# Transposing x in blocks of two tokens of one head, with the states doubled in place of a copy that pairs heads

## The chip, the cores and the metric

The kernel runs on one core of a Trainium2 chip. A core has five engines with queues of their own: TensorE (PE in the profile; its weight loads have a row of their own, PEld), VectorE (DVE), ScalarE (ACT), GpSimd (POOL) and SyncE (SP, which here only issues DMAs). TensorE reads SBUF and writes PSUM, eight banks of 2 KB per partition. The metric is the device time of one execution in microseconds (us). Inputs are float32, the arithmetic is bfloat16 with sums in float32.

## The reference

There are B = 8 batches, H = 8 heads, S = 512 tokens, Ns = 32 states, and D = 64 elements per head. A block of cross attention between tokens and states is followed by a feed-forward layer with an exact GELU.

```python
scores = scale * x @ state^T          # per batch and head: 512 x 32
a = exp(scores - max); a /= a.sum(-1) + 1e-09
xread = a @ state                     # 512 x 64
scores2 = scale * state @ x^T         # 32 x 512, softmax over the tokens
sread = a2 @ x                        # 32 x 64
attn = concat([xread, sread], axis=2) # 544 rows per batch and head
x = attn, heads side by side          # (8 * 544) x 512
out = gelu(x @ w_in) @ w_out          # w_in 512 x 2048, w_out 2048 x 512
```

## The kernel before, in words

The order of the work is written out by hand (`tc.manual_schedule()`): each engine runs its instructions in the order in which the code issues them, and waits on semaphores where data come from another engine or a DMA. There is no planner.

**Per batch.** For the rows of tokens the kernel never forms xread. It multiplies each head's states with that head's 64 rows of w_in first (`p_mm`, L435: the tile `P`, 32 states of 4 heads = 128 rows, for two groups of heads t = 0, 1, by 2048 columns) and then multiplies the transposed attention weights `AT` with P (`mm1`, L501, called as `M`): a block of 128 of the 2048 hidden columns by 512 tokens, two matmuls of 512 columns, then one GELU on ScalarE into `g`. The heads are numbered h = 4 t + c, with t the half (0 or 1) and c = 0 to 3. The second product, g by w_out, is made for batches 1 to 7 with seven half-size products in place of eight (`X(b, "1")` to `X(b, "7")`, L672), whose operands are sums and differences that VectorE makes (`g_sum`, L629, and `w_diff`, L563); one quarter of that is cut once more (`sub_a`, `sub_b`, L736 and L743). Results leave by DMAs from SyncE's queue.

**Scores and softmax.** `scores(b, half)` (L325) makes 8 matmuls of 64 columns: the stationary operand is a 128 x 128 block of x transposed, the moving operand 64 columns of `sbd`, a table of the states in which two 64 x 32 blocks stand on a diagonal and the rest is zero. The exponential on ScalarE follows, and `norm` on VectorE (a sum, a reciprocal, and a product of two SBUF operands: L353, L355, L356). The state reads (`reads_mm`, L955) need x with a column of ones beside it, `xo`, which `rearr_ones` (L230) copies from x.

**How x comes in.** `load_x(b)` (L115) is a DMA issued from GpSimd's queue that converts to bfloat16. It fills `xb`: 128 partitions, 8 heads, and per head 4 tokens of 64 elements side by side. There are two buffers. In `scores` a block of x transposed holds one token of two heads, c of t = 0 and c of t = 1. In `xb` the 64 elements of those two heads lie far apart. So `rearr(b)` (L221) copies them together into `x4` on GpSimd, two copies of 1024 elements per partition for each of batches 2 to 7, and `xtr_dma(b)` (L276) transposes x4 into `xT` by one DMA transpose from SyncE's queue. Batch 1 is transposed on TensorE (`xtr`, L264): 32 transposes of 64 columns each, into the two partition halves of PSUM, and two copies by VectorE. Batch 0 has a path of its own.

**How the states come in.** `load_st` (L120) loads the states of batch 1, of batch 2, and of batches 3 to 7 at three places, as `st_bf`: 128 partitions (4 heads by 32 states), the two halves t side by side. `state_prep(b0, b1)` (L156) makes one TensorE transpose for each batch and two VectorE copies into the diagonal blocks of `sbd`; it is called for batch 1 at L1134, batch 2 at L1187, and batches 3 to 7 together at L1218. `sbd` is set to zero once at the start on GpSimd (L95).

**The order around the change.** Batches 0 and 1 are woven together by hand (L1074 to L1220). From there each batch b = 2 to 7 has eight slots p = 0 to 7 (loop at L1222). Every slot holds two blocks of M and one product X of the batch before; the scores of the next batch stand in slot 1, its softmax in 2 and 3, the DMA transposes in 3 and 5, its P and state reads in slot 5 (`p_all`, L986, copies at L1002), the small products of `sub_a` and `sub_b` in 5 and 6. GpSimd's queue carries loads and copies; a one-element copy `hold_for` (L1015) makes it wait for a given block of g, so that a load doesn't start earlier. PSUM tiles named "f" take four buffers in turn, the others fixed banks.

**Other uses of the buffers.** The two x4 buffers later hold sums of w_in for the rows of states (`sr_w`, L814, products "1" and "6") and the last sum of g (L1320).

Of the kernel before, what the change touches and what calls it, by code (L numbers as in the profile page):

```python
# [17 lines left out]
def kernel(  # L18
# [49 lines left out]
    ident = persist.tile([128, 128], BF16, name="ident")  # L68
    sbd = persist.tile([128, B, HC, 2 * NS], BF16, name="sbd")
    XSR = persist.tile([128, HC, NS, B], BF16, name="XSR")  # L70
# [4 lines left out]
    x0b = persist.tile([128, 4, SJ, 2, D], BF16, name="x0b", tag="mix1")  # L75
    xT0 = persist.tile([128, 4, SJ, 128], BF16, name="xT0", tag="mix2")
    sb0 = persist.tile([128, 2, 2, 2, NS], BF16, name="sb0")
    hold = persist.tile([128, 1], BF16, name="hold")
    spare = persist.tile([128, 1], FP32, name="spare")
    warm = persist.tile([128, 512], BF16, name="warm")  # L80
    xos = [persist.tile([128, SJ, HC, 132], BF16, name=f"xo_{i}") for i in range(2)]
    x4s = [persist.tile([128, SJ, HC, 128], BF16, name=f"x4_{i}") for i in range(2)]

# [10 lines left out]

    nc.gpsimd.memset(sbd, 0.0)  # L95
    xbs = {}
# [37 lines left out]
    def load_rest():  # L134
        load_w_out(4, 6)
        load_w_out(6, 8)
        load_w_in(1024, 1536)
        load_w_out(8, 12)
        load_w_in(1536, 2048)
        load_st(2, 3)  # L140
        load_x(2)
        load_w_out(12, 16)
        load_x(3)


# [8 lines left out]


    def state_prep(b0, b1, pool=ps_f, tag="f"):  # L156
        n = b1 - b0
        ps = pool.tile([128, n, HC, NS], BF16, name="st_ps", tag=tag)
        for b in range(b0, b1):
            nc.tensor.transpose(  # L160
                ps[:, b - b0, :, :].rearrange("p c n -> p (c n)"),
                st_bf[:, b, :, :].rearrange("q t d -> q (t d)"),
                ident,
            )
        for t in range(2):
            nc.vector.tensor_copy(
                out=sbd[64 * t:64 * t + 64, b0:b1, :, 32 * t:32 * t + 32].rearrange(
                    "d b c n -> d (b c) n"
                ),
                in_=ps[64 * t:64 * t + 64, :, :, :].rearrange("d b c n -> d (b c) n"),  # L170
            )
# [23 lines left out]
    def state0_p(ps):  # L195
        for t in range(2):
            h = slice(64 * t, 64 * t + 64)
            nc.scalar.copy(out=sbd[h, 0, :, 32 * t:32 * t + 32], in_=ps[h, 2, :, :])

# [6 lines left out]
    def begin(b):  # L206
        A = Att()
        atts[b] = A
        A.x4 = x4s[b % 2]
        A.xo = xos[b % 2]  # L210
        if b > 0:
            A.xT = att.tile([128, SJ, HC, 128], BF16, name="xT", tag="xT")

# [5 lines left out]


    def rearr(b, ts=(0, 1)):  # L221
        A = atts[b]
        src = xbs[b].rearrange("p (t c) (j d) -> p t c j d", t=2, d=D)
        for t in ts:
            nc.gpsimd.tensor_copy(  # L225
                out=A.x4[:, :, :, 64 * t:64 * t + 64].rearrange("p j c d -> p c j d"),
                in_=src[:, t],
            )

# [33 lines left out]

    def xtr(b, cs):  # L264
        A = atts[b]
        xv = xbs[b].rearrange("p (t c) (j d) -> p j c t d", t=2, d=D)
        ps = ps_f.tile([128, len(cs), SJ, 128], BF16, name="xT_ps", tag="f")
        for i, c in enumerate(cs):
            for j in range(SJ):
                for t in range(2):  # L270
                    nc.tensor.transpose(ps[64 * t:64 * t + 64, i, j, :], xv[:, j, c, t, :], ident)
        nc.vector.tensor_copy(
            out=A.xT[:, :, cs[0]:cs[0] + len(cs), :].rearrange("p j c n -> p c j n"), in_=ps
        )
# [50 lines left out]
    def scores(b, half):  # L325
        A = atts[b]
        if half == 0:
            begin_e(b)
        pt = ps_f.tile([128, SJ, 2, 2, NS], FP32, name="pt", tag="f")
        for ci in range(2):  # L330
            c = 2 * half + ci
            for j in range(SJ):
                nc.tensor.matmul(  # L333
                    pt[:, j, :, ci, :],
                    lhsT=A.xT[:, j, c, :],
                    rhs=sbd[:, b, c, :],
                    start=True,
                    stop=True,
                )
# [95 lines left out]
    def p_mm(b, f, tiles):  # L435
# [44 lines left out]
    def pmat00(h):  # L480
# [3 lines left out]
        for c in range(HC):  # L484
            for t in range(2):
                nc.tensor.matmul(
                    ps[t][32 * c:32 * c + 32, :],
                    lhsT=sbd[64 * t:64 * t + 64, 0, c, 32 * t:32 * t + 32],
                    rhs=w_in_bf[64 * t:64 * t + 64, c, 256 * h:256 * h + 256],
# [324 lines left out]
    def sr_w(name):  # L814
        if name in "52":
            homes = [opool.tile([128, 2, 512], BF16, name="srw", tag="osb") for _ in range(2)]
        elif name == "7":
            t = att.tile([128, 2, 2, 512], BF16, name="srw7", tag="xT")
            homes = [t[:, 0], t[:, 1]]
        else:  # L820
            t = x4s["16".index(name)].rearrange("p j c n -> p (j c n)")
            t = t.rearrange("p (g k f) -> p g k f", g=2, k=2)
            homes = [t[:, 0], t[:, 1]]
        (h0, k0), (h1, k1), op = G_SUMS[name]
# [307 lines left out]
    mm2_m(0, 0)  # L1132
    mm2_m(0, 1)
    state_prep(1, 2)  # L1134
    mm2_m(0, 2)
# [4 lines left out]
    begin(1)  # L1140
    xtr(1, (0, 1))
    xtr(1, (2, 3))
    sread(0)
# [31 lines left out]
    begin(2)  # L1175
    rearr(2)
    xtr_dma(2)
    begin(3)
    rearr(3)
    rearr_ones(3)  # L1180
# [31 lines left out]
    for f, t, ps in ((0, 1, p0), (0, 0, p0), (1, 0, p1)):  # L1212
        nc.vector.tensor_copy(out=Ps[2][:, t, f * 512:(f + 1) * 512], in_=ps[t])
    M(28, 29)
    hold_for(1, 12)
    rearr_ones(2)
    M(30, 31)
    state_prep(3, B)  # L1218
    snap(1, "c2", "c2", xs[1, 0])
    X(1, "4")  # L1220

    for b in range(2, B):  # L1222
        nb = b + 1
        for p in range(8):
# [68 lines left out]
            if p == 5:  # L1293
# [25 lines left out]
    X(b, "6")  # L1319
    g_sum(b, "3", x4s[0].rearrange("p j (u c) n -> p (j u) (c n)", u=2))  # L1320
    R("3")
# [35 lines left out]
```

## Time and profile before

| | before |
|---|---|
| median of 3 runs | 201.92 us (201.89 to 202.7) |
| the profiled execution | 202.25 us, span 200.3 us |
| TensorE busy | 193.9 us (97%) |
| VectorE busy | 155.1 us (77%) |
| ScalarE busy | 145.6 us (73%) |
| GpSimd busy | 48.1 us (24%) |
| pairing copies on GpSimd (L225) | 12 copies, 1040 ns each |
| transposes of x of batch 1 (L271) | 32, 1.08 us of the chain |
| transposes of the states (L160) | 1, 1 and 5 |

Times count from the start of the span. The profile of one execution is read in parts: busy time by engine; the chain, which goes back from the last instruction to what released it, and so on; groups of instructions with their mean time and what ended the idle time before them; and the timeline. The share of the span by engine is an average over stages. In a row of the timeline a number ahead of the brackets is the start, then the duration; the brackets hold the idle time of that engine just before and what ended it. A matmul's record is longer than the pace at which matmuls follow each other, since they are pipelined: a 128 x 128 transpose has a record of 219 ns, and eight of them take 0.45 us in the chain.

### The profile page before, as it was taken

The page shows a single profiled execution, that of the slowest core. Times are in us where ns is not written, and L with a number is a line of the kernel's source. Part 1 is how long each engine was busy: PE and PEld are TensorE (multiplying, and loading weights), DVE is VectorE, ACT ScalarE, POOL GpSimd, SP SyncE. Part 2 cuts the span into 40 slices and gives each one's busy share as a digit, 9 for nine tenths or more (in the row PEclk, how much of TensorE's full clock was granted, in tenths as well). Part 3 has the DMA queues.
Part 4 walks back from the last instruction along what each step waited for, and adds up shares of the span by engine and source line. Part 5 has one row for each costly group of instructions (what it writes and reads, how often), then busy time and mean ns, then how long its engine had stood idle before and what let it go on. Part 6 is the DMA issues. An engine that isn't in the chain of part 4 may idle for free.

```text
span 200.3 us, 5055 instructions
## 1 busy us (share of the span) xinstructions
PE 193.9 (97%) x2102; PEld 134.3 (67%) x2107; DVE 155.1 (77%) x279; ACT 145.6 (73%) x264; POOL 48.1 (24%) x65
## 2 busy tenths in 40 slices
PE   7899999999999999999999999999999999999993
PEld 2533544465767777767777787677776888878893
DVE  2963796969989769975997798849966897984863
ACT  3785577699896799569966997599948778775120
POOL 8972504543403444040504300030000000000000
PEclk9999999999999999999999999999999999999999
DMA  5999999976494959680797025420024010030044
GB/s 192 197 174 202 206 199 201 183 136 142 84 149 77 241 65 164 141 214 0 77 188 209 5 67 95 138 75 27 28 107 106 0 55 0 7 153 0 18 146 157
DMA packets 40567, 23.16 MB, mean 116 GB/s; under 512 B 21856, under 2 KB 39136, under 8 KB 40544
## 3 DMA queue, kind: packets, MB, share of 16 engines
q0 software_dynamic: 13984, 8.10, 29.9%
q1 hardware_dynamic: 25728, 14.22, 27.5%
q10 hardware_dynamic: 832, 0.52, 0.8%
q8 instruction: 16, 0.26, 0.5%
q14 instruction: 7, 0.06, 0.1%
HBM read 17.30 MB, written 8.91 MB: 131 GB/s over the span
## 4 chain that ended last, share of the span: by engine, by line
PE 86%; DMA 5%; POOL 4%; ACT 2%; issue 0%; DVE 0%; POOLq 0%
PE xp L647 36%; PE hp L506 26%; DMA xb<-in_x_dram 5%; PE xp L727 5%; PE op L548 3%; PE sp L866 3%; PE rp L932 3%; POOL w_in_bf L105 2%; PE op L532 2%; PE xp L773 2%; PE pt L333 2%; ACT P L1002 1%; PE p_ps L441 1%; PE sr L962 1%; POOL sbd L95 1%; POOL w_out_bf L113 1%
## 5 line engine op out<-in xcount | busy, mean ns | idle before, releaser
L513 ACT ACTIVATE g<-hp 128x512 bf16<-128x512 f32 x124 | 67.1, 614 | 17.0 <-PE hp L506 16.8
L506 PE MATMUL hp<-AT,P 128*128 128x512 bf16 x248 | 62.2, 379 | 0.0
L647 PEld LDWEIGHTS <-gsum 128*128 128x128 bf16 x416 | 40.4, 98 | 8.9 <-issue 0.4
L647 PE MATMUL xp<-ws,gsum 128*128 128x256 bf16 x320 | 38.2, 273 | 0.0
L506 PEld LDWEIGHTS <-P 128*128 128x128 bf16 x248 | 23.0, 98 | 19.4 <-ACT P L452 0.7
L647 PEld LDWEIGHTS <-g 128*128 128x128 bf16 x240 | 23.3, 98 | 4.8
L637 DVE TENSOR_TENSOR gsum<-g 128x2048 bf16<-128x2048 bf16 x14 | 17.0, 1218 | 0.6 <-ACT g L513 0.6
L225 POOL COPY x<-xb 128x1024 bf16<-128x1024 bf16 x12 | 12.2, 1044 | 18.5 <-DMA xb<-in_x_dram 18.5
L235 POOL COPY xo<-xb 128x1024 bf16<-128x1024 bf16 x12 | 12.2, 1043 | 14.1 <-PE sr L962 13.9
L647 PE MATMUL xp<-w_out_bf,g 128*128 128x256 bf16 x128 | 15.3, 273 | 0.0
L647 PE MATMUL xp<-ws,g 128*128 128x256 bf16 x112 | 13.4, 273 | 0.0
L1016 POOL COPY hold<-g 128x1 bf16<-128x1 bf16 x7 | 2.3, 334 | 42.9 <-ACT g L513 42.9
L666 DVE TENSOR_TENSOR c<-qb 128x256 f32<-128x256 f32 x6 | 2.6, 425 | 12.7 <-ACT qb L749 12.7
L548 PE MATMUL op<-w_out_bf,g 128*128 128x512 bf16 x44 | 11.0, 380 | 0.5 <-issue 0.3
L647 PE MATMUL xp<-w_out_bf,gsum 128*128 128x256 bf16 x96 | 11.5, 273 | 0.0
L666 DVE TENSOR_TENSOR oh<-xp,c 128x512 f32<-128x512 f32 x14 | 9.6, 686 | 2.4 <-PE xp L647 2.0
L1002 DVE CAST P<-p_ps 128x512 bf16<-128x512 f32 x15 | 9.4, 683 | 2.4 <-PE p_ps L441 2.4
L356 DVE TENSOR_TENSOR a<-e,ics 128x512 bf16<-128x512 bf16 x14 | 10.5, 750 | 0.5
L353 DVE TENSOR_REDUCE cs<-e 128x16 f32<-128x512 bf16 x14 | 9.5, 678 | 0.9 <-ACT e L340 0.9
L513 ACT ACT_TABLE_LOAD x7 | 9.0, 1283 | 0.1
L441 PE MATMUL p_ps<-w_in_bf,sbd 64*32 64x512 bf16 x248 | 9.0, 380 | 0.0
L637 DVE TENSOR_TENSOR gsum<-gsum,g 128x2048 bf16<-128x2048 bf16 x7 | 8.6, 1225 | 0.2
(155 smaller groups left out, 308.9 us busy)
## 6 DMA issues: line engine op xcount, KB each, us to landing
out_dram<-oh SPq DMA_DIRECT2D x15, 256.0 KB, 3.3
xb<-in_x_dram POOLq DMA_DIRECT2D x7, 512.0 KB, 7.1
out_dram<-oh SPq DMA_DIRECT2D x6, 512.0 KB, 3.1
w_in_bf<-in_moe_w_in_dram POOLq DMA_DIRECT2D x6, 256.0 KB, 11.7
out_dram<-osb SPq DMA_DIRECT2D x5, 256.0 KB, 3.0
w_out_bf<-in_moe_w_out_dram POOLq DMA_DIRECT2D x4, 256.0 KB, 7.8
w_out_bf<-in_moe_w_out_dram POOLq DMA_DIRECT2D x2, 512.0 KB, 13.3
x0f<-in_x_dram SPq DMA_DIRECT2D x3, 256.0 KB, 3.8
```

The costliest lines, as they stand in the source:

```text
L225: nc.gpsimd.tensor_copy(out=A.x4[:, :, :, 64 * t:64 * t + 64].rearrange("p j c d -> p c j d"), in_=src[:, t],)
L235: eng.tensor_copy(out=A.xo[:, :, :, 2 + 64 * t:66 + 64 * t].rearrange("p j c d -> p c j d"), in_=src[:, t],)
L356: nc.vector.tensor_tensor(out=A.a[:, :, hs].rearrange("p g (c n) -> p g c n", n=NS), in0=e4, in1=ics[:, :, :].to_broadcast((128, G, 2, NS) ...
L441: nc.tensor.matmul(ps[t][32 * c:32 * c + 32, :], lhsT=sbd[64 * t:64 * t + 64, b, c, 32 * t:32 * t + 32], rhs=w_in_bf[64 * t:64 * t + 64, c ...
L506: nc.tensor.matmul(hp, lhsT=Ps[b][:, t, m * 128:(m + 1) * 128], rhs=atts[b].AT[:, :, t, :], start=(t == 0), stop=(t == 1),)
L513: nc.scalar.activation(out=gs[b][:, m, :], in_=hp, func=AF.Gelu)
L548: nc.tensor.matmul(ops[b, j], lhsT=gs[b][:, m, j * 128:(j + 1) * 128], rhs=w_out_bf[:, m, :], start=(m == 0), stop=(m == MC - 1),)
L637: nc.vector.tensor_tensor(out=got[name], in0=x, in1=y, op=op)
L647: nc.tensor.matmul(ps[:, j - js[0], :], lhsT=lhs[:, m, 128 * j:128 * j + 128], rhs=rhs[:, m, :], start=(first and j == js[0] and m == 0), ...
L666: nc.vector.tensor_tensor(out=out, in0=x, in1=y, op=ALU.add)
L727: nc.tensor.matmul(xs[b, 0][:, at, :], lhsT=lhs[:, m, :], rhs=rhs[:, m, :], start=(start and m == 0), stop=(m == MH // 2 - 1), skip_group_ ...
L1002: copy(out=Ps[b][:, t, f * 512:(f + 1) * 512], in_=ps[t])
```

## The change

A block of x transposed now holds two tokens of one head in place of one token of two heads. In `xb` those 128 elements lie side by side, so the DMA transpose reads `xb` itself, and `rearr` and the x4 buffers go. `xT` becomes [128, head, pair of tokens, 128]. The moving operand must then hold the same head's states twice on the diagonal, so `sbd` has an entry for each of 8 heads in place of 4 pairs (twice the size), and a new tile `st2` holds each state twice side by side before it is transposed. `state_twice` makes those copies: for batch 1 on VectorE, for 2, for 3, and for 4 to 7 on GpSimd. `state_prep` makes two transposes for each batch in place of one, with copies of twice the size; batches 4 to 7 move from L1218 to slot 6 of batch 2. The count of matmuls in `scores` stays, in the order c, t, pair of tokens. Half of `sbd` is set to zero at the start, half behind the load of x of batch 3. Batch 1 is transposed in 16 full transposes. The later users of x4 move to a new tile `late4`, to `st_bf`, and to a buffer of the `a` tiles.

```diff
-    sbd = persist.tile([128, B, HC, 2 * NS], BF16, name="sbd")
+    sbd = persist.tile([128, B, H, 2 * NS], BF16, name="sbd")
...
+    st2 = persist.tile([128, B - 4, 2, 2, D], BF16, name="st2")
...
-    x4s = [persist.tile([128, SJ, HC, 128], BF16, name=f"x4_{i}") for i in range(2)]
+    late4 = persist.tile([128, 4, 512], BF16, name="late4")
...
-    nc.gpsimd.memset(sbd, 0.0)
+    nc.gpsimd.memset(sbd[:, 0:B // 2], 0.0)
...
         load_x(3)
+        nc.gpsimd.memset(sbd[:, B // 2:B], 0.0)
+        state_twice(2, 3, nc.gpsimd)
...
+    def state_twice(b0, b1, eng):
+        eng.tensor_copy(
+            out=st2[:, b0 % 4:b0 % 4 + b1 - b0].rearrange("q b t u d -> q (b t) u d"),
+            in_=st_bf[:, b0:b1].rearrange("q b t d -> q (b t) d")[:, :, None, :].broadcast_to(
+                [128, 2 * (b1 - b0), 2, D]
+            ),
+        )
+
     def state_prep(b0, b1, pool=ps_f, tag="f"):
...
-        ps = pool.tile([128, n, HC, NS], BF16, name="st_ps", tag=tag)
-        for b in range(b0, b1):
-            nc.tensor.transpose(
-                ps[:, b - b0, :, :].rearrange("p c n -> p (c n)"),
-                st_bf[:, b, :, :].rearrange("q t d -> q (t d)"),
-                ident,
-            )
-        for t in range(2):
+        ps = pool.tile([128, n, H, NS], BF16, name="st_ps", tag=tag)
+        for b in range(n):
+            for t in range(2):
+                nc.tensor.transpose(
+                    ps[:, b, HC * t:HC * t + HC, :].rearrange("p c n -> p (c n)"),
+                    st2[:, (b0 + b) % 4, t].rearrange("q u d -> q (u d)"),
+                    ident,
+                )
+        for u in range(2):
             nc.vector.tensor_copy(
-                out=sbd[64 * t:64 * t + 64, b0:b1, :, 32 * t:32 * t + 32].rearrange(
-                    "d b c n -> d (b c) n"
+                out=sbd[64 * u:64 * u + 64, b0:b1, :, 32 * u:32 * u + 32].rearrange(
+                    "d b h n -> d (b h) n"
                 ),
...
-    def rearr(b, ts=(0, 1)):
-        A = atts[b]
-        src = xbs[b].rearrange("p (t c) (j d) -> p t c j d", t=2, d=D)
-        for t in ts:
-            nc.gpsimd.tensor_copy(
-                out=A.x4[:, :, :, 64 * t:64 * t + 64].rearrange("p j c d -> p c j d"),
-                in_=src[:, t],
-            )
...
-    def xtr(b, cs):
+    def xtr(b, hs):
         A = atts[b]
-        xv = xbs[b].rearrange("p (t c) (j d) -> p j c t d", t=2, d=D)
-        ps = ps_f.tile([128, len(cs), SJ, 128], BF16, name="xT_ps", tag="f")
-        for i, c in enumerate(cs):
-            for j in range(SJ):
-                for t in range(2):
-                    nc.tensor.transpose(ps[64 * t:64 * t + 64, i, j, :], xv[:, j, c, t, :], ident)
...
+        ps = ps_f.tile([128, len(hs), SJ // 2, 128], BF16, name="xT_ps", tag="f")
+        for i, h in enumerate(hs):
+            for q in range(SJ // 2):
+                nc.tensor.transpose(ps[:, i, q, :], xbs[b][:, h, 128 * q:128 * q + 128], ident)
+        nc.vector.tensor_copy(out=A.xT[:, hs[0]:hs[0] + len(hs)], in_=ps)
...
         nc.sync.dma_start_transpose(
-            out=A.xT.rearrange("p j c n -> p (j c) n"),
-            in_=A.x4.rearrange("p j c n -> p (j c n)"),
+            out=A.xT.rearrange("p h q n -> p (h q) n"),
+            in_=xbs[b].rearrange("p h d -> p (h d)"),
         )
...
         for ci in range(2):
-            c = 2 * half + ci
-            for j in range(SJ):
...
+            for t in range(2):
+                h = HC * t + 2 * half + ci
+                for q in range(SJ // 2):
+                    nc.tensor.matmul(
+                        pt[:, 2 * q:2 * q + 2, t, ci, :],
+                        lhsT=A.xT[:, h, q, :],
+                        rhs=sbd[:, b, h, :],
...
-                    lhsT=sbd[64 * t:64 * t + 64, b, c, 32 * t:32 * t + 32],
+                    lhsT=sbd[64 * t:64 * t + 64, b, HC * t + c, 32 * t:32 * t + 32],
...
+        elif name == "6":
+            homes = [
+                st_bf.rearrange("q (k b) t d -> q k (b t d)", k=2),
+                att.tile([128, 2, 512], BF16, name="srw6", tag="a"),
+            ]
...
     mm2_m(0, 1)
+    state_twice(1, 2, nc.vector)
     state_prep(1, 2)
...
-    xtr(1, (0, 1))
-    xtr(1, (2, 3))
+    xtr(1, range(0, 4))
+    xtr(1, range(4, 8))
...
     begin(2)
-    rearr(2)
     xtr_dma(2)
     begin(3)
-    rearr(3)
     rearr_ones(3)
...
     M(28, 29)
+    state_twice(3, 4, nc.gpsimd)
     hold_for(1, 12)
...
-    state_prep(3, B)
+    state_prep(3, 4)
...
                 load_x(4 if b == 2 else b + 3)
+                if b == 2:
+                    state_twice(4, B, nc.gpsimd)
...
                 begin(nb + 1)
-                rearr(nb + 1)
...
             if p == 6:
+                if b == 2:
+                    state_prep(4, B)
                 sub_b(b)
```

More of the change, by code (lines that the diff above doesn't have):

```diff
@@ L153, in keep_warm @@
             n -= 4
+    def state_twice(b0, b1, eng):
[5 more added lines that the diff above has]
+        )
     def state_prep(b0, b1, pool=ps_f, tag="f"):
         n = b1 - b0
-        ps = pool.tile([128, n, HC, NS], BF16, name="st_ps", tag=tag)
-        for b in range(b0, b1):
-            nc.tensor.transpose(
-                ps[:, b - b0, :, :].rearrange("p c n -> p (c n)"),
-                st_bf[:, b, :, :].rearrange("q t d -> q (t d)"),
-                ident,
-            )
-        for t in range(2):
+        ps = pool.tile([128, n, H, NS], BF16, name="st_ps", tag=tag)
[7 more added lines that the diff above has]
+        for u in range(2):
             nc.vector.tensor_copy(
-                out=sbd[64 * t:64 * t + 64, b0:b1, :, 32 * t:32 * t + 32].rearrange(
-                    "d b c n -> d (b c) n"
+                out=sbd[64 * u:64 * u + 64, b0:b1, :, 32 * u:32 * u + 32].rearrange(
+                    "d b h n -> d (b h) n"
                 ),
-                in_=ps[64 * t:64 * t + 64, :, :, :].rearrange("d b c n -> d (b c) n"),
+                in_=ps[64 * u:64 * u + 64, :, :, :].rearrange("d b h n -> d (b h) n"),
             )
@@ L197, in state0_p @@
             h = slice(64 * t, 64 * t + 64)
-            nc.scalar.copy(out=sbd[h, 0, :, 32 * t:32 * t + 32], in_=ps[h, 2, :, :])
+            nc.scalar.copy(out=sbd[h, 0, HC * t:HC * t + HC, 32 * t:32 * t + 32], in_=ps[h, 2, :, :])
     class Att:
@@ L208, in begin @@
         atts[b] = A
-        A.x4 = x4s[b % 2]
         A.xo = xos[b % 2]
         if b > 0:
-            A.xT = att.tile([128, SJ, HC, 128], BF16, name="xT", tag="xT")
+            A.xT = att.tile([128, H, SJ // 2, 128], BF16, name="xT", tag="xT")
     def begin_e(b):
@@ L261, in xtr0 @@
         copy(out=xT0[:, q, :, :], in_=ps)
-    def xtr(b, cs):
+    def xtr(b, hs):
         A = atts[b]
-        xv = xbs[b].rearrange("p (t c) (j d) -> p j c t d", t=2, d=D)
-        ps = ps_f.tile([128, len(cs), SJ, 128], BF16, name="xT_ps", tag="f")
-        for i, c in enumerate(cs):
-            for j in range(SJ):
-                for t in range(2):
[L271 to L274, printed above, removed]
+        ps = ps_f.tile([128, len(hs), SJ // 2, 128], BF16, name="xT_ps", tag="f")
[3 more added lines that the diff above has]
+        nc.vector.tensor_copy(out=A.xT[:, hs[0]:hs[0] + len(hs)], in_=ps)
     def xtr_dma(b):
@@ L330, in scores @@
         for ci in range(2):
-            c = 2 * half + ci
-            for j in range(SJ):
[L333 to L339, printed above, removed]
+            for t in range(2):
[5 more added lines that the diff above has]
+                        rhs=sbd[:, b, h, :],
+                        start=True,
+                        stop=True,
+                    )
         nc.scalar.activation(
@@ L487, in pmat00 @@
                     ps[t][32 * c:32 * c + 32, :],
-                    lhsT=sbd[64 * t:64 * t + 64, 0, c, 32 * t:32 * t + 32],
+                    lhsT=sbd[64 * t:64 * t + 64, 0, HC * t + c, 32 * t:32 * t + 32],
                     rhs=w_in_bf[64 * t:64 * t + 64, c, 256 * h:256 * h + 256],
@@ L820, in sr_w @@
         else:
-            t = x4s["16".index(name)].rearrange("p j c n -> p (j c n)")
-            t = t.rearrange("p (g k f) -> p g k f", g=2, k=2)
-            homes = [t[:, 0], t[:, 1]]
+            homes = [late4[:, 0:2], late4[:, 2:4]]
         (h0, k0), (h1, k1), op = G_SUMS[name]
@@ L1319 @@
     X(b, "6")
-    g_sum(b, "3", x4s[0].rearrange("p j (u c) n -> p (j u) (c n)", u=2))
+    g_sum(b, "3", late4.rearrange("p k (u n) -> p (k u) n", u=2))
     R("3")
```

## The prediction

> **What bounds the kernel now.** I read the page's busy shares first, then the chain that ended last, then that chain in order of time, and only then the rows of the instructions that are edited. The profiled execution took 202.25 us, of which 200.3 us are the span and 1.95 us lie around it; the three timed runs have a median of 201.92 us, so this execution stands 0.33 us above it. I make the sum on the profiled execution and carry the difference over to the median.
>
> ```profile
> span 200.3 us, 5055 instructions
> ...
> PE 193.9 (97%) x2102; PEld 134.3 (67%) x2107; DVE 155.1 (77%) x279; ACT 145.6 (73%) x264; POOL 48.1 (24%) x65
> ...
> PEclk9999999999999999999999999999999999999999
> ...
> PE 86%; DMA 5%; POOL 4%; ACT 2%; issue 0%; DVE 0%; POOLq 0%
> ```
>
> TensorE is busy for 97% of the span at full granted clock, and it holds 86% of the chain. GpSimd (POOL) is busy for 24%, VectorE (DVE) holds none of the chain. So what is taken off GpSimd or VectorE has no price of its own; a TensorE instruction added after the start has its full price.
>
> The chain in order of time, at the three places that the change touches on TensorE:
>
> ```profile
> 9.01 10.36 DMA xb<-in_x_dram
> ...
> 19.41 1.08 PE xT_ps L271 x32
> ...
> 21.39 0.47 PE pt L333 x16
> ...
> 38.64 0.06 PE st_ps L160
> ...
> 48.47 0.28 PE st_ps L160 x5
> ...
> 68.44 0.86 PE hp L506 x4
> 69.30 0.67 PE xp L727 x12
> ```
>
> Up to 19.41 the end is set by the load of x of batch 1, not by TensorE; afterwards the pieces of TensorE follow each other without a hole, so each us there is a us of the end. The only other things in the chain after that are five short ScalarE waits, one in slot 5 of each of batches 2 to 6 (at 66.4 to 67.4 the first of them).
>
> **The change part by part.**
>
> *The pairing copies.* Twelve copies of 1040 ns on GpSimd go (12.5 us). Nothing on TensorE waits for GpSimd in that time: the DMA transposes that read their result land well ahead. That of batch 2 is issued at 34.19 and lands 6.6 us later, at 40.8, before its scores at 41.98; that of batch 4 lands at 66.4 for scores at 75.0. They now start up to 2 us earlier: gain 0. That of batch 3 is issued at 48.06 behind the transpose of batch 2's weights, not behind a copy, and lands 4.6 us later, at 52.7, for scores at 52.95: it stays where it is, with 0.2 us to spare.
>
> *What they cost VectorE.* These rows show it:
>
> ```profile
> 61.30 1.83 DVE L637 TENSOR_TENSOR gsum<-g,gsum 128x2048 bf16<-128x2048 bf16 x1
> ...
> 76.93 2.07 POOL L225 COPY x<-xb 128x1024 bf16<-128x1024 bf16 x2 [1.77 <-DMA xb<-in_x_dram]
> ...
> 78.04 1.51 DVE L356 TENSOR_TENSOR a<-e,ics 128x512 bf16<-128x512 bf16 x1
> ```
>
> An addition that takes 1.22 us elsewhere takes 1.83 here, and a product of 0.69 us takes 1.51: it ends 0.55 us after the copy beside it. VectorE operations with two inputs in SBUF stand while GpSimd copies. That goes too, some 3 us of VectorE. But no matmul after 27 us waits for one of these operations, so I price it at 0.
>
> *xT of batch 1.* 32 transposes of 64 columns become 16 of 128. Their starts show that the old ones run in pairs, 55 ns from pair to pair; eight full-width transposes of the attention weights take 0.45 us, 56 ns each. So 16 x 56 = 0.90 stands against 16 x 55 = 0.88: no gain, though half the instructions go. Dependency: the first half of the scores used the first of two VectorE copies of xT; it now takes heads 0, 4, 1, 5 in this order, so its third matmul waits for the second copy. That copy ends at 21.38, the first matmul is at 21.23. The third would start near 21.5 in place of 21.3: 0.2 us, of which the next transpose (it waits until 21.83 for VectorE) and the reads at 24.58 (they wait for ScalarE, 0.09 us) take most. I take 0; bounds 0 and 0.2.
>
> *State of batch 1.* VectorE first doubles it (128x256). VectorE is idle from 13.6 to 15.4 and the state landed at 11.2 (6.4 plus 4.8), so that is done before TensorE comes at 14.84. One more transpose, 0.06, and two larger copies: 64x128 takes about 0.22 us, 64x640 about 0.48, so 64x256 near 0.29. Together 0.2 us later for the P matmuls that wait for them at 16.07, and for all behind them, up to xT_ps at 19.41, where TensorE now waits 0.23 us for x. I take 0; bounds 0 and 0.2.
>
> *States of batches 2 to 7 on TensorE.* Batch 2: two transposes for one, +0.06. At 48.47: two for five, -3 x 0.056 = -0.17. New in slot 6 of batch 2, between the matmuls at 68.44 and those at 69.30: eight, +0.45. All lie in the unbroken part of the chain: +0.34.
>
> *The copies behind those eight.* By the same two rows 64x1024 takes about 0.70 us, two 1.4 us, on VectorE from about 70.0 to 71.4. VectorE is idle there: its row before says so.
>
> ```profile
> 71.54 0.42 DVE L666 TENSOR_TENSOR c<-qb 128x256 f32<-128x256 f32 x1 [1.92 <-ACT qb L749]
> ```
>
> It waits 1.92 us for ScalarE, so the three additions queued behind the copies are hardly later. Were they 1 us late, the sum for X(2,"6") would be ready at 76.15 and that product starts at 76.14: slack of 1 us. Price 0, up to 0.3. The new PSUM tile takes the fourth buffer of the rotation, which VectorE emptied at 67.6.
>
> *GpSimd's doubling copies.* By 1040 ns for 1024 elements: 0.3 us for batch 2 (the state lands at 29.4, used at 38.3) and for batch 3 (load near 40, plus 5.0 us, so about 45, used at 48.1), and 1.04 us for batches 4 to 7 right behind the load of x of batch 4, near 53.8. There VectorE starts a weight difference of 1.22 us at 53.83, which may stand for 1 us; VectorE has 0.71 us idle at 60.1, before two P copies used at 62. Price 0, up to 0.2.
>
> *Queues.* On POOL's queue the load of states 3 to 7 stands behind the ones copy and a wait for xT of batch 2; it goes out up to 2 us earlier. The load of x of batch 4 gains a wait for the transpose of batch 3 (landed at 52.7, the load goes at 52.89). On SP's queue the transposes wait for the load in place of the copy. The first one now runs beside the last weights (landing at 34.6, used at 36.25) and x of batch 3 (37.3, needed 2 us later for the same order of things as now): 0.
>
> *The second half of the memset.* The table of states doubles; half is set at the start with the old 2048 elements (1.80 us), the other half right behind the load of x of batch 3, at 24.85 to 26.65. Beside it, in the old trace:
>
> ```profile
> 23.95 0.88 POOL L117 DMA_DIRECT2D xb<-in_x_dram  x1 [1.28 <-DVE xo L235]
> 24.97 0.69 DVE L356 TENSOR_TENSOR a<-e,ics 128x512 bf16<-128x512 bf16 x1
> 25.58 0.68 DVE L453 CAST P<-p_ps 128x512 bf16<-128x512 f32 x1
> 26.16 1.03 PE L506 MATMUL hp<-AT,P 128*128 128x512 bf16 x4
> ```
>
> The row at 24.97 is of the form that stood for a GpSimd copy, the cast is queued behind it, and the matmuls at 26.16 wait for the cast. If a memset holds VectorE as a copy does, the product ends at 26.65 + 0.55 = 27.2 in place of 25.6, and TensorE loses 1.6 us. If not, 0. No row shows a memset beside such an operation; the nearest is the first memset, beside which five small VectorE memsets run at 60 to 72 ns each without a pause. A memset reads nothing, and what stood before was a second input. I take 0 and keep 1.6 as the end.
>
> The Trainium skill ("SBUF — State Buffer", Who interferes with whom) says that a VectorE operation with two SBUF inputs contends with a GpSimd instruction that reads SBUF, and not with one that only writes it; the copies above agree with the first half (1.51 against 0.69 us), no row here shows the second. By that page the memset costs 0 and the sum stays; by the copies' rows it would be 1.6 us more.
>
> **Sum.** 0.06 - 0.17 + 0.45 = +0.34 on 202.25, or 202.59 for the profiled execution; on the median, 201.92 + 0.34 = 202.26 us. The likeliest case's own range: below, -0.2 if the added transposes partly fall into waits and the runs vary downwards (201.7); above, the bounds 0.2 + 0.2 + 0.3 + 0.2 do not add, I allow 0.5 of their 0.9 (202.8).
>
> **The rivals.** (a) *The memset stops VectorE*, and through it the P cast and M(8), at 25 us: 201.92 + 0.34 + 1.6 = 203.86. It speaks for it that GpSimd's copies do just that; against it that a memset has no input. It decides from 0.66 us of lost matmul time on. (b) *VectorE's relief reaches the end.* The five waits of slot 5, about 0.45 us each beyond the pace of the matmuls, are 2.2 us; with two thirds gone, 201.92 + 0.34 - 1.5 = 200.8. Against it: they are waits for ScalarE (sraw, P), and ScalarE's rows there wait for TensorE, never for VectorE. (c) *A transfer is late.* If the earlier transpose of batch 2 or the later order on POOL's queue pushes states 3 to 7 by more than the 3 us to spare at 48.1, TensorE stands: each us beyond is a us, say 203.3. Against it: both are released earlier, not later.
>
> **How the numbers follow.** Likeliest 0.75, (a) 0.12, (b) 0.08, (c) 0.05. Half a per cent (1.0 us) is about what a measurement can tell from no change; the likeliest lies inside it, (a) and (c) above, (b) below: 0.08, 0.75, 0.17. The range takes the likeliest case's 201.7 to 202.8 and reaches to 201.4, where over half of (b)'s gain lies, and to 203.4, over (c) and where two thirds of (a)'s loss lie; what it leaves out, most of (a) and of (b), is under 2 in 10.
>
> **What would show it.** In the new profile: the 16 transposes at 19.4 still take about 0.9 us; eight st_ps in a row near 69 for 0.45 us; the product near 24.97 at 0.69 us beside the memset (then (a) is wrong) or above 1.5 us; no VectorE product of 1.5 us at 78; the slot 5 waits unchanged. I am wrong if xT_ps starts later than 19.6, or if a wait for VectorE or a load shows in TensorE's rows after 27 us.

## The result, and the profile after

The changed kernel takes 202.55 us (median; 202.25 to 203.26) beside 201.94 us for the kernel before, measured in turn with it. The ratio is 1.0026, with a 95% interval of 1.0015 to 1.0037: +0.52 us, from 0.30 to 0.75. That is a small loss inside the half per cent that the prediction called "no change". The forecast was 202.26 us, in a range of 201.4 to 203.4. The profiled execution took 202.55 us with a span of 200.5 us, against 202.25 and 200.3 before.

From the page of the kernel after: the span, busy time by engine, the granted clock in forty slices, and the chain's shares by engine.

```profile
span 200.5 us, 5046 instructions
...
PE 194.6 (97%) x2098; PEld 134.4 (67%) x2098; DVE 154.4 (77%) x282; ACT 145.4 (73%) x264; POOL 40.4 (20%) x57
...
PEclk9999999999999999999999999999999999999999
...
PE 91%; ACT 3%; DMA 2%; DVE 1%; issue 0%; SPq 0%
```

GpSimd lost 7.7 us and VectorE 0.7 us; TensorE, already busy for 97% of the span, gained 0.7 us, and the time went up. The chain still is TensorE's. Here it is in order of time (start, duration, what), at the start and at the places that the change touches:

```profile
1.25 4.49 DMA x0f<-in_x_dram
...
17.99 1.50 PE hp L505 x6
19.50 0.94 PE xT_ps L271 x16
...
21.33 0.62 PE pt L332 x16
...
38.58 0.11 PE st_ps L172 x2
...
48.48 0.11 PE st_ps L172 x2
...
67.15 1.05 PE xp L726 x16
68.20 0.86 PE hp L505 x4
69.06 0.45 PE st_ps L172 x8
69.51 0.67 PE xp L726 x12
```

The two new st_ps at 38.58 take 0.11 in place of 0.06; the two at 48.48 stand where five took 0.28; the eight in a row at 69.06 take 0.45, between the same two neighbours that touched each other before (68.44 + 0.86 = 69.30). The chain's beginning is different: up to 19.5 it runs through batch 0's own loads and TensorE's work for batch 0, while before it ran through the load of x of batch 1. Which of the two is the later one differs from run to run: of two kernels below that both have the old start, one's chain begins with the load of x of batch 1, the other's with batch 0's own way.

To separate the start from the rest I use marks in the trace: the first matmuls of the scores of batches 1, 2, 3 and 4, the last matmul, and the end of the span. All are first starts in TensorE's records, in us, and the columns are differences between neighbouring marks. (The end of the span is taken to the nanosecond here; the expectations quoted below took it in tenths of a us, so their ends differ by up to 0.05.)

| kernel | scores 1 at | 1 to 2 | 2 to 3 | 3 to 4 | 4 to last matmul | scores 1 to last | last matmul to end |
|---|---|---|---|---|---|---|---|
| before | 21.23 | 20.75 | 10.97 | 22.08 | 122.04 | 175.84 | 3.24 |
| after | 21.17 | 20.81 | 10.80 | 22.46 | 122.03 | 176.10 | 3.24 |
| after, second profile | 20.79 | 20.87 | 10.85 | 22.45 | 122.04 | 176.21 | 3.22 |
| before + eight transposes | 20.61 | 21.09 | 10.97 | 22.46 | 122.04 | 176.56 | 3.28 |
| after, states of 4 to 7 by DMA | 21.57 | 20.81 | 10.83 | 22.00 | 122.04 | 175.68 | 3.58 |
| the same, second profile | 20.94 | 20.81 | 10.84 | 22.01 | 122.04 | 175.70 | 3.57 |
| after, batch 1 as before | 21.24 | 20.82 | 10.80 | 22.44 | 122.04 | 176.10 | 3.23 |
| after, zeros copied | 20.87 | 22.35 | 10.85 | 22.46 | 122.04 | 177.70 | 3.22 |
| after, copies put back | 21.68 | 20.82 | 10.84 | 22.45 | 122.03 | 176.14 | 3.24 |
| after, states of 2 to 7 by DMA | 20.92 | 20.71 | 10.81 | 22.00 | 122.04 | 175.56 | 3.52 |
| before + one DMA | 20.83 | 20.76 | 10.96 | 22.00 | 122.04 | 175.76 | 3.63 |
| states 2 to 7 by DMA, two DMAs fewer | 20.86 | 20.70 | 10.81 | 22.00 | 122.03 | 175.54 | 3.15 |

The second column moves by a whole us between profiles, and not with the kernel. The others repeat to a few hundredths, at worst 0.1 us, for the same TensorE work, far better than whole runs do (a kernel's runs spread over a us). There is one exception, the 21.09 in the fourth row, which is followed up below. In them the change is plain. From the scores of batch 1 to the last matmul, the kernel before and the one that only adds a DMA need 175.84 and 175.76. The four profiles with the changed kernel's TensorE work (after twice, batch 1 as before, copies put back) need 176.10, 176.21, 176.10 and 176.14. The means differ by 0.34 us: +0.06 or a little more between batches 1 and 2, -0.11 to -0.17 between 2 and 3, and 22.45 against 22.00 or 22.08 between 3 and 4.

The remaining claims of the prediction are read in the timeline of the kernel after (start, duration, engine, operation; in brackets the idle time ahead of it and what ended it):

```profile
24.77 1.83 POOL L145 MEMSET sbd<- 128x2048 bf16 x1
24.92 0.69 DVE L355 TENSOR_TENSOR a<-e,ics 128x512 bf16<-128x512 bf16 x1
...
25.52 0.68 DVE L452 CAST P<-p_ps 128x512 bf16<-128x512 f32 x1
...
51.46 1.23 DVE L636 TENSOR_TENSOR gsum<-gsum,g 128x2048 bf16<-128x2048 bf16 x1
51.59 1.15 POOL L1018 COPY hold<-g 128x1 bf16<-128x1 bf16 x1 [1.23 <-ACT g L512]
...
53.05 0.69 DVE L665 TENSOR_TENSOR oh<-xp,c 128x512 f32<-128x512 f32 x1 [0.36 <-PE xp L646]
...
53.66 2.27 DVE L575 TENSOR_TENSOR ws<-w_out_bf 128x2048 bf16<-128x2048 bf16 x1
53.79 1.05 POOL L160 COPY st<-st_bf 128x1024 bf16<-128x1024 bf16 x1
...
69.62 1.39 DVE L178 COPY sbd<-st_ps 64x1024 bf16<-64x1024 bf16 x2 [0.24 <-PE st_ps L172]
...
71.30 0.43 DVE L665 TENSOR_TENSOR c<-qb 128x256 f32<-128x256 f32 x1 [0.30 <-ACT qb L748]
...
78.25 0.69 DVE L355 TENSOR_TENSOR a<-e,ics 128x512 bf16<-128x512 bf16 x1
```

Beside the memset the product takes its usual 0.69 us, and the cast behind it starts at once. Beside GpSimd's doubling copy the weight difference takes 2.27 us in place of 1.22, longer by the whole copy (1.05). Its record starts 0.13 us ahead of the copy's, but VectorE's instruction before it ends only at 53.74, 0.05 us ahead of the copy, so which of the two was first isn't clear. At 51.46, where VectorE had nothing else under way, it is the other way round: the sum takes its usual 1.23 us, and GpSimd's one-element copy behind it takes 1.15 us in place of 0.19. The copies behind the eight transposes take 1.39 us and end at 71.0, and the addition at 71.30 still waits for ScalarE. The product at 78.25, which took 1.51 us before, takes 0.69.

### The profile page after: what moved, and what is told of

The parts are those of the page before. It is cut to its first block, busy times and chain, and to the rows that moved or that the text cites. A ratio compares the mean times of both kernels' runs of the same rounds, so it can differ in the third digit from the quotient of the medians.

```text
span 200.5 us, 5046 instructions
## 1 busy us (share of the span) xinstructions
PE 194.6 (97%) x2098; PEld 134.4 (67%) x2098; DVE 154.4 (77%) x282; ACT 145.4 (73%) x264; POOL 40.4 (20%) x57
## 4 chain that ended last, share of the span: by engine, by line
PE 91%; ACT 3%; DMA 2%; DVE 1%; issue 0%; SPq 0%
PE xp L646 36%; PE hp L505 27%; PE op L547 5%; PE xp L726 5%; PE sp L868 3%; PE rp L934 3%; DMA x0f<-in_x_dram 2%; PE op L531 2%; PE xp L772 2%; PE pt L332 2%; PE p_ps L440 2%; ACT P L1004 1%; PE sr L964 1%; PE hp L1116 1%; PE aT_ps L373 1%; ACT g L512 1%
## 5 line engine op out<-in xcount | busy, mean ns | idle before, releaser
L1018 POOL COPY hold<-g 128x1 bf16<-128x1 bf16 x7 | 3.0, 431 | 46.8 <-ACT g L512 46.8
L547 PE MATMUL op<-w_out_bf,g 128*128 128x512 bf16 x48 | 11.8, 380 | 0.0
L355 DVE TENSOR_TENSOR a<-e,ics 128x512 bf16<-128x512 bf16 x14 | 9.7, 692 | 0.5
L451 ACT CAST P<-p_ps 128x512 bf16<-128x512 f32 x9 | 4.9, 590 | 4.8 <-PE p_ps L440 4.8
```

The lines of the kernel that those rows point to most:

```text
L355: nc.vector.tensor_tensor(out=A.a[:, :, hs].rearrange("p g (c n) -> p g c n", n=NS), in0=e4, in1=ics[:, :, :].to_broadcast((128, G, 2, NS) ...
L547: nc.tensor.matmul(ops[b, j], lhsT=gs[b][:, m, j * 128:(j + 1) * 128], rhs=w_out_bf[:, m, :], start=(m == 0), stop=(m == MC - 1),)
```

## The experiments

The theory on trial (T in the texts below): the end follows TensorE's instructions, so the difference is that of its transposes, +0.34 us. Its rivals were those of the prediction (the memset, VectorE's relief, a late transfer) and, since the timed +0.52 lies above +0.34, one more (U in the texts below): the longer way of batch 1's states and scores makes the start later. A last one, L, came from the experiments themselves.

**The same kernel again.** No edit; timed beside the experiments that follow.

> The changed kernel once more, beside the kernel before and the three experiments that follow, so that all stand on one chip. Theory T (the loss is TensorE's added transposes behind 19.4 us, 0.06 - 0.17 + 0.45 = +0.34 us, all else is hidden): +0.3 to +0.4 us on before. Rival U (besides, the longer path of batch 1 ahead of 19.4 us, 0.3 us in the profile, shows wherever x of batch 1 lands early): +0.5 to +0.65 us.

202.16 us beside 201.91; ratio 1.002 (1.0001 to 1.0038), or +0.4 us (0.02 to 0.77). The loss is there again, with +0.34 well inside.

**The eight transposes alone.** To the kernel before, in slot 6 of batch 2, eight transposes are added whose result is thrown away, with a tiny copy by VectorE that frees the buffer.

```diff
             if p == 6:
+                if b == 2:
+                    more = ps_f.tile([128, 8, 128], BF16, name="more_ps", tag="f")
+                    for i in range(8):
+                        nc.tensor.transpose(
+                            more[:, i, :], st_bf[:, 4 + i // 2, :, :].rearrange("q t d -> q (t d)"), ident
+                        )
+                    nc.vector.tensor_copy(out=spare2, in_=more[:, :, 0])
```

> The kernel before, with eight further transposes of states in slot 6 of batch 2 at the place where the change puts its eight; their result is thrown away. T and U both: +0.45 us on before, since TensorE has no wait there. A rival V (the eight partly fall into a wait of TensorE, or ScalarE sets the pace behind them): +0.2 us or less.

202.52 us beside 201.91; ratio 1.0034 (1.0012 to 1.0055), or +0.7 us (0.24 to 1.1). Its chain in order of time:

```profile
68.09 0.86 PE hp L507 x4
68.96 0.45 PE more_ps L1313 x8
69.40 0.67 PE xp L728 x12
```

From the scores of batch 3 to those of batch 4 it needs 22.46 us, as the kernel after does, against 22.00 or 22.08 without the eight. So they have their full price, and no wait behind them takes any of it. In the whole time +0.46 lies inside the interval. (Its stretch from batch 1 to 2 is longer by 0.33 us in this one profile, ahead of the edit. Its trace shows three pauses of 0.11 to 0.12 us there. TensorE was 0.6 us earlier than in the kernel before, but two loads of w_out were not: one landed at 27.44, and the matmul that waited for it starts at 27.48; the other landed at 34.93, and VectorE stood 1.07 us for it, so that a transpose at 38.09 and a matmul at 38.69 waited for VectorE. Before, these loads landed at 26.72 and 34.60, and TensorE's matmuls do not show these pauses. So here half of what an early start gained was lost again to loads.)

**The eight transposes taken off TensorE.** In the kernel after, the states of batches 4 to 7 are transposed by one DMA from SyncE's queue, from `st2` into `late4` (`state_dma`), and VectorE makes its two copies into `sbd` from there in place of PSUM (`state_spread`).

```diff
                 if b == 2:
                     state_twice(4, B, nc.gpsimd)
+                    state_dma(4, B)
...
                 if b == 2:
-                    state_prep(4, B)
+                    state_spread(4, B)
```

> The changed kernel with the eight transposes taken off TensorE: the doubled states of batches 4 to 7 go through one DMA transpose on SyncE's queue behind the doubling copy (near 55 us), and VectorE copies them into the table at the same place as now, from SBUF in place of PSUM. T: -0.45 us on the changed kernel, so about -0.1 us on before. U: -0.45 us on the changed kernel too, so +0.1 to +0.2 us on before. V: -0.2 us or less on the changed kernel. If the DMA transpose delays that of x of batch 4 or the results behind it, a wait shows in TensorE's rows near 75 us.

202.45 us beside 201.91; ratio 1.0031 (1.0011 to 1.0052), where about -0.1 was expected. This was a miss, and a useful one, because TensorE did what was asked of it. The chain in order of time no longer has st_ps there:

```profile
68.62 0.86 PE hp L528 x4
69.48 0.67 PE xp L749 x12
```

The stretch from batch 3 to 4 fell to 22.00, and from the scores of batch 1 to the last matmul it needs 0.16 us less than before. Yet the kernel was slower. In the table two columns stand out: the scores of batch 1 began late in this profile (21.57), and the end behind the last matmul took 3.58 us in place of 3.24. A second set of runs of the same kernel was to tell the two apart.

> The kernel with the DMA transpose for batches 4 to 7 once more. Its profile had 0.5 us less TensorE work than the changed kernel's and its time was no shorter; in that execution the last piece of x of batch 0 landed 5.9 us after its issue, against 4.6 before. If that start is an accident of one execution, the median now lies at 201.6 to 201.9 us. If it belongs to this kernel, it lies at 202.3 or more again, and its profile again starts the scores of batch 1 later than 21.4.

202.33 us beside 201.88; ratio 1.002 (1.0005 to 1.0035). This time the start was not late (20.94), so the first time's late start was an accident; but the time stayed above the 201.6 to 201.9 expected for that case, and the end took 3.57 us again. What the longer end is, the last two experiments show.

**Batch 1 as before.** In the kernel after, batch 1 alone keeps its old form: one state transpose without the doubling, 32 transposes of 64 columns, and scores in the old order (`state_pair1` and `xtr_pair1` are the old `state_prep` and `xtr`).

```diff
-    state_twice(1, 2, nc.vector)
-    state_prep(1, 2)
+    state_pair1()
...
-    xtr(1, range(0, 4))
-    xtr(1, range(4, 8))
+    xtr_pair1((0, 1))
+    xtr_pair1((2, 3))
```

> The changed kernel with batch 1 alone as before: x in blocks of two heads by 32 half transposes, its states by one transpose without doubling, its scores from pairs. T: the same as the changed kernel within 0.1 us. U: 0.2 to 0.3 us faster than the changed kernel.

202.27 us beside 201.91; ratio 1.0017 (1.0001 to 1.0033), and 176.10 us from the scores of batch 1 to the last matmul, exactly as the kernel after. So batch 1's new way costs nothing that these runs can see. The times alone, each with an interval of 0.3 to 0.4 us to either side, would not rule out the 0.2 us of rival U; the traces do: from TensorE's first `op` matmul to batch 1's P matmuls it is 2.75 us before and 2.81 after, which is the one transpose more, and from the first transpose of x to the first scores 1.82 and 1.80.

**Zeros by a copy.** The second half of the memset becomes a GpSimd copy of zeros from another tile, of the same size and at the same place. The instruction takes about as long (1.90 us in place of 1.83), but now it reads SBUF.

```diff
-        nc.gpsimd.memset(sbd[:, B // 2:B], 0.0)
+        nc.gpsimd.tensor_copy(
+            out=sbd[:, B // 2:B].rearrange("p b h n -> p b (h n)"),
+            in_=warm[:, None, :].broadcast_to([128, B // 2, 512]),
+        )
```

> The changed kernel with the second half of the table set to zero by a GpSimd copy of a tile of zeros in place of the memset: the same 2048 elements at the same place in GpSimd's queue (near 24.8 us), but GpSimd now reads SBUF. If what holds VectorE's two-input product is GpSimd's reading, the product near 24.9 us, 0.69 us beside the memset, stands until the copy's end: a copy of 2048 elements takes about 2.05 us by the rows of 1024, so it ends near 26.8, the product near 27.4, the P cast behind it starts 1.8 us later, and the whole run is 1.5 to 1.8 us longer than the changed kernel. If the product only happened to win the race for the port, or the cast isn't on the path: no difference.

203.73 us beside 201.88; ratio 1.0091 (1.0074 to 1.0108). From the scores of batch 1 to the last matmul it needs 177.70 us, 1.5 to 1.6 more than the kernel after, and the stretch from batch 1 to 2 holds nearly all of it (22.35 against 20.81). The timeline of this kernel:

```profile
24.51 1.90 POOL L145 COPY sbd<-warm 128x2048 bf16<-128x2048 bf16 x1
24.62 2.35 DVE L358 TENSOR_TENSOR a<-e,ics 128x512 bf16<-128x512 bf16 x1
...
26.89 0.68 DVE L455 CAST P<-p_ps 128x512 bf16<-128x512 f32 x1
...
27.63 1.69 PE L508 MATMUL hp<-AT,P 128*128 128x512 bf16 x7 [1.45 <-DVE P L455]
```

The product starts 0.11 us after the copy and ends 0.56 us after the copy's end; the cast queued behind it is late, and TensorE stands for 1.45 us. This is rival (a) as the prediction described it, with its price of 1.6 us, and it shows that the place was dangerous: the change is spared because its instruction there is a memset and not a copy. The Trainium skill ("SBUF — State Buffer", Who interferes with whom) says that a VectorE operation with two SBUF inputs contends with a GpSimd instruction that reads SBUF and not with one that only writes it. The runs agree with both halves now: 0.69 us beside the memset, 2.35 beside the copy.

**The pairing copies put back.** The kernel after, with GpSimd's twelve copies at their old places, into `late4`, where nothing reads them. This gives VectorE its old delays again and leaves the rest.

```diff
+    def rearr(b):
+        src = xbs[b].rearrange("p (t c) (j d) -> p t c j d", t=2, d=D)
+        for t in range(2):
+            nc.gpsimd.tensor_copy(
+                out=late4.rearrange("p j (c n) -> p j c n", c=HC)[:, :, :, 64 * t:64 * t + 64].rearrange("p j c d -> p c j d"),
+                in_=src[:, t],
+            )
...
+    rearr(2)
...
+    rearr(3)
...
+                rearr(nb + 1)
```

> The changed kernel with the twelve pairing copies put back at their old places on GpSimd (1024 elements each, into a tile that nobody reads then); the transposes still read x itself. Theory (VectorE's relief is worth nothing at the end): the same as the changed kernel within 0.15 us, though VectorE's two-input operations beside the copies take 1.5 to 2 us again. Rival (the relief hides a part of the loss): 0.3 us or more slower than the changed kernel.

202.33 us beside 201.88; ratio 1.0028 (1.0005 to 1.005). In its timeline the product stands again:

```profile
78.71 2.48 POOL L235 COPY late<-xb 128x1024 bf16<-128x1024 bf16 x2 [2.37 <-DMA xb<-in_x_dram]
78.80 1.50 DVE L363 TENSOR_TENSOR a<-e,ics 128x512 bf16<-128x512 bf16 x1
```

From the scores of batch 1 to the last matmul it needs 176.14 us, as the kernel after does. GpSimd's 12.5 us and VectorE's waits beside them were worth nothing that these marks could show (0.1 us): rival (b) falls.

**All states of batches 2 to 7 by DMA.** If TensorE's instructions set the end, taking the rest of the state transposes off it should help. The states of batches 2 and 3 are loaded together and take the same way as those of 4 to 7.

```diff
-        load_st(2, 3)
+        load_st(2, 4)
...
-        state_twice(2, 3, nc.gpsimd)
+        state_twice(2, 4, nc.gpsimd)
+        state_dma(2, 4)
...
-    state_prep(2, 3, ps_o, "o3")
+    state_spread(2, 4)
...
-    state_twice(3, 4, nc.gpsimd)
-    state_prep(3, 4)
```

> The changed kernel with all states of batches 2 to 7 transposed by DMA: those of batches 2 and 3 loaded together, doubled on GpSimd near 29 us and sent through a DMA transpose ahead of that of x of batch 2; those of 4 to 7 as in the experiment before. No state transpose is left on TensorE behind 19.4 us. From the scores of batch 2 to the last matmul: 0.37 + 0.11 = 0.5 us less than the changed kernel, 0.17 + 0.08 = 0.25 us less than the kernel before, 0.06 + 0.11 of it ahead of batch 3's scores. In time about 0.3 us below the kernel before, if the DMAs near 30 us (weights, x of batch 3) are not delayed so far that TensorE waits for the last weights near 36 us.

202.09 us beside 201.88; ratio 0.9995 (0.9978 to 1.0013): no difference, where about 0.3 us less was expected. Its TensorE work from the scores of batch 1 on is 175.56 us, 0.2 to 0.3 below the kernel before, and its end takes 3.52 us, 0.3 more. VectorE gains too: the same two copies take 0.85 us out of SBUF, against 1.39 us out of PSUM in the kernel after:

```profile
68.96 0.85 DVE L204 COPY sbd<-late 64x1024 bf16<-64x1024 bf16 x2
```

**One DMA more, and nothing else.** The longer end appeared in just those kernels that issue one or two DMAs more (49 and 50 from SyncE and ScalarE, in place of 48). In the traces every DMA that SyncE or ScalarE issues signals one of eight semaphores, in turn: 100, 102, 103, 105, 106, 116, 117, 118, and 100 again. At the end SyncE waits for all of them, in this same order in all twelve traces. Theory L: the end is longer because the last transfer of the kernel now falls on a semaphore early in that order, and all the waits behind it come after. To try this without the rest, the kernel before issues one DMA more early on, where a result tile of batch 0 leaves in two halves.

```diff
-            h = d_model // 2 if j == SJ - 1 else d_model
+            h = d_model // 2 if j >= SJ - 2 else d_model
```

> The kernel before with one change only: the third result tile of batch 0 leaves in two DMAs of half its width in place of one (near 44 us), so that there is one DMA more on the queues of SyncE and ScalarE. The two kernels with DMA transposes for the states ended 3.52 to 3.56 us after their last matmul began, all others 3.20 to 3.28. Theory L: at the end SyncE waits for the semaphores of the eight DMA lanes in a fixed order, about 65 ns each; with one DMA more the last transfer's lane moves from the last place of that order to the second, and eight waits stand behind it in place of none. Then the end lies 0.3 us later here too (3.55), and the time is 0.3 us above before. Rival: the longer end belongs to the DMA transposes; then 3.2 to 3.3 and no difference in time.

202.25 us beside 202.0; ratio 1.0023 (1.0004 to 1.0041). Its matmuls take 175.76 us (175.84 before), its end 3.63 us (3.24). These are SyncE's last waits out of the two traces: the time at which each wait was over, and the two semaphores that it names; the one of the last transfer is marked.

```
before                        one DMA more
197.59  115, 114              197.10  115, 114
197.65  100, 113              198.91  100, 113   <- last transfer
197.72  102, 112              198.97  102, 112
197.78  103, 111              199.03  103, 111
197.84  105, 110              199.09  105, 110
198.48  106, 109              199.15  106, 109
199.02  116, 108              199.21  116, 108
199.19  117, 101              199.27  117, 101
199.40  118, 107  <- last     199.33  118, 107
```

In both kernels the last transfer is signalled 1.75 us after its issue (197.65 to 199.40; 197.16 to 198.91). Before, its wait is the last; only the steps that close every one of these programs follow, 0.9 us in both traces. With one DMA more it is the second, and seven waits of 0.06 us (not eight, as was expected) follow it: 0.42 us. The profile shows the same in the waits of SyncE's queue in the last 8 us (total, times, longest), first of the kernel before, then with one DMA more:

```profile
SPq L1352 <- DMA out_dram<-oh: 1.2, 3, 0.6
```

```profile
SPq L1352 <- DMA out_dram<-oh: 1.8, 1, 1.8
```

Three waits that follow the landings one by one have become a single one that holds up all the others.

**Two DMAs fewer.** If that is so, the version with all states by DMA should win once its last transfer is back on semaphore 118. Two DMAs are merged into others: the last result tile of batch 0 leaves in one piece, and so does a result of batch 1 that left in two.

```diff
-            h = d_model // 2 if j == SJ - 1 else d_model
+            h = d_model
...
-            x_out(b, 0, left)
+            if b > 1:
+                x_out(b, 0, left)
...
-            x_out(b, 0, right)
+            x_out(b, 0, right if b > 1 else slice(None))
```

> The kernel with DMA transposes for the states of batches 2 to 7, and two DMAs fewer elsewhere: the last result tile of batch 0 leaves in one DMA in place of two halves, and two quarter results of batch 1 leave together. The count of DMAs on the two queues is the same as in the kernel before. Theory L: the end is 3.2 to 3.3 us after the last matmul again; 155.08 - 154.86 = 0.2 us less than before from the scores of batch 2 to the last matmul, 0.3 us less than the kernel without this edit; 201.6 to 201.7 us, faster than both kernels. Rival: the end stays at 3.5 us, and the time at 201.9 to 202.1.

201.75 us beside 202.0; ratio 0.9984 (0.9972 to 0.9996), or -0.3 us (-0.6 to -0.1). SyncE's queue waits in three pieces again:

```profile
SPq L1381 <- DMA out_dram<-oh: 1.1, 3, 0.6
```

Its matmuls take 175.54 us from the scores of batch 1 on (0.2 to 0.3 less than before) and its end 3.15 us. It keeps the change's blocks of x and its saved copies, takes the states' transposes of batches 2 to 7 off TensorE, and is faster than the kernel before by 0.2%, and so than the kernel after (1.0026 against the same kernel before). That it is faster than the version with two DMAs more is shown by the marks of the end (3.15 against 3.52), not by the times, whose intervals overlap.

## Why the prediction was right, point by point

The forecast of 202.26 and the "no change" were right, and for the reason given: TensorE's instructions after the start have their full price, and nothing else in the change has one that shows.

- **The eight transposes, +0.45.** The chain shows 0.45, and the stretch that holds them is longer by 0.37 against the profile before and by 0.45 against the five others without them (22.00). The eight alone, in the kernel before, lengthen it to the same 22.46. Full price.
- **Batch 3, -0.17, and batch 2, +0.06.** The stretches show -0.11 to -0.17 and +0.06 to +0.12. The sum of +0.34 is the +0.34 between the means of the profiles; that they agree to the hundredth is luck, since profiles with the same TensorE work differ by 0.1. The timed +0.52 (0.30 to 0.75) holds it; the 0.2 us between the two are within the measurement and have no place in the traces behind the start. Whether the start is later by so much isn't settled: it varies by a us from profile to profile, in all kernels.
- **xT of batch 1, 0.** 16 transposes take 0.94 us in the chain where 32 took 1.08; in the marks, from the first of them to the first scores, it is 1.80 after and 1.82 before. The third scores matmul does wait for the second copy, 0.15 us where at most 0.2 was allowed, and TensorE has it back before 24.6.
- **Batch 1's states, 0 with a bound of 0.2.** The measured delay is 0.06, and undoing batch 1's whole change moved nothing that can be measured. The reason given, that TensorE waits there for x of batch 1 anyway, does not always hold: in the second profile of the kernel after, x landed at 18.94 and TensorE came to it at 19.00, straight from the work before it, so that the 0.06 is not hidden there.
- **The copies behind the eight.** They take 1.39 us where 1.4 was worked out, and end 0.3 us before VectorE has anything else to do.
- **GpSimd's doubling copies.** The weight difference at 53.66 takes 1.05 us more, as said, and no matmul is later for it.
- **The memset, 0 or 1.6.** It is 0 for a memset and 1.5 to 1.6 for a copy at the same place. The condition of rival (a) was the right one, and the forecast decided rightly by the missing input.
- **VectorE's relief, 0.** It shows at 78.25 (0.69 in place of 1.51), and putting the copies back changes nothing. VectorE's busy time fell by 0.7 us and not by some 3, since the change also gives it a doubling copy, larger copies into `sbd`, and the 1.05 us at 53.66. Rival (b) is false.
- **Late transfers.** No wait for a load or a DMA transpose shows in TensorE's chain after the start. The transpose with the least room, of x of batch 3, landed at 52.39 for scores at 52.78. Rival (c) is false.
- **The range.** The lower end of the likeliest case, 201.7, lies 0.56 us below the sum; the text names 0.2 of that and leaves the rest to the scatter of the runs without a number. Nothing here hangs on it.

What failed was not in the prediction but in the expectation of the DMA experiment: moving work from TensorE to a DMA was taken to be free as long as nobody waits for that DMA. It wasn't, because the added DMA also moved the last transfer to another semaphore.

## What to carry to other kernels

Where one engine's instructions follow each other without a hole, price a change by the instructions that it adds to that engine, and not by what it takes off the others, unless one of its instructions waits for them: 12.5 us of GpSimd copies were worth nothing that showed, and 0.34 us of TensorE did. When a wait or an overlap decides, look for what an instruction reads: a memset and a copy of zeros at the same place differ by 1.6 us. And with whole runs spread over a us, compare marks inside the trace, from more than one profile: here they mostly repeated to hundredths, and they show at once whether a difference lies in the start, in the work or in the end.

## What was unexpected of the hardware

The end of this kernel depends on how many DMAs SyncE and ScalarE issue. The eight semaphores are waited for in a fixed order at 0.06 us each. With 48 DMAs the last transfer is on the last of them, and the span ends 3.15 to 3.28 us after the last matmul's start; with 49 or 50 it is 3.52 to 3.63. Since the semaphores are used in turn, the count modulo eight should decide, but no other counts were run. These waits are instructions that stand in the program's trace, so this is a matter of how the program is built as much as of the chip. In the time the one DMA alone was worth +0.2% (ratio 1.0023, 1.0004 to 1.0041), as much as the change itself.

Where VectorE's operation with two SBUF inputs and a GpSimd copy overlap, either can stand for the other. At 53.66 VectorE lost the whole 1.05 us of the copy. At 51.46, with VectorE 0.13 us ahead, GpSimd's one-element copy stood for VectorE, 1.15 us in place of 0.19, and again at 74.05, where VectorE was 0.36 us ahead (0.91). That the one that starts first goes first fits these rows, but the order at 53.66 is too close to read, and it wasn't tried.
